# Another order of the steps in the opening of an attention and FFN kernel

## The chip, the cores and the metric

The kernel runs on one core of a Trainium2 chip. The core has engines that work side by side, each on its own row of instructions: TensorE for matmuls (PE in the profile, its weight loads PEld), VectorE (DVE), ScalarE (ACT), GpSimd (POOL) and SyncE (SP), which here only issues DMAs. An engine takes its instructions strictly in the order in which the program lists them; an instruction whose data isn't there yet holds up everything behind it on that engine. The metric is the device time of one launch in microseconds.

## What is computed

Attention with keys and values that are averaged over groups of 8 positions, then layer norm and a feed-forward network with a residual:

```python
B, H, S, D = 8, 8, 576, 64                     # q, k, v in float32
k_p = k.reshape(B, H, S // 8, 8, D).mean(axis=3)
v_p = v.reshape(B, H, S // 8, 8, D).mean(axis=3)
scores = np.matmul(q, k_p.transpose(0, 1, 3, 2)) / np.sqrt(D)
attn = softmax(scores)
x = concat_heads(np.matmul(attn, v_p))         # (8, 576, 512)
xn = (x - mean(x)) / np.sqrt(var(x) + 1e-06) * g_ln
out = x + np.maximum(xn @ w_ch1, 0.0) @ w_ch2  # 512 -> 2048 -> 512
```

## The kernel before

The 4608 tokens are 36 tiles of 128, and four tiles make a chunk of 512 rows of the FFN. Every float32 operand of a matmul is split into two float16 parts, hi and lo, and each product is three matmuls (hi by hi, hi by lo, lo by hi). The first two chunks run the FFN plainly; from the third on a scheme with seven products in place of eight takes over. The weights w1 and w2 arrive as raw 1 MB blocks, eight each, and are made into scaled float16 pairs on the chip. The opening does all of this at once, from about 0 to 230 us: the attention of the first tiles, the making of both weights, the plain FFN of two chunks, and the sums of weights that the seven products need.

What sets the order is written out by hand. Each piece of work is a generator, and a table of tokens drives it: every time that a token appears in the table, its generator runs on to its next `yield` and so adds its next few instructions to the rows of the engines; a token whose generator has ended does nothing.

```python
for token in tokens.split():
    if token not in begun:
        name, *args = token.split(".")
        begun[token] = iter(ops[name](*map(int, args)) or ())
    next(begun[token], None)
```

There are two tables: START for the opening, of some 760 tokens, and STEADY for the rest. The tokens that matter here:

- A.t: scores of tile t (PE L790, maximum and subtraction on DVE L800 and L805, exponentials and float16 parts on ACT L814 to L819 and POOL L826, L829, then a transpose by DMA on SP, L837). E.t.h does the transposing of the first four tiles on PE.
- B.t: attention times values (PE L928 to L930 for the first batch, L932 and L933 later, with `va` and `vb`; sums and statistics on DVE L939 to L961, normalising on POOL L968 and L987, float16 parts and a transpose for the FFN, L1083 to L1090). Tiles 0 to 3 are transposed on PE (L881, L889).
- HV.b.h, HK.b.h: load and average values and keys of a batch. D.b: four DMAs on SP (L757, L758) that spread the values of batch b into `va` and `vb`. HV.1.1's last steps make those values (ACT L483 into `vh`, DVE L490 into `vb`).
- R.m.b: the load of raw block b of weight m (SP L510). C.m.b: its conversion (ACT L535 and L539, DVE L527 and L543; for w2 the maximum on ACT L553). M1.h, M2.h: the scale of half h of a weight (a chain on DVE with one matmul, PE L470).
- S.m.b: the split of block b into float16 hi and lo. It writes over the place of block b - 1, so the splits of a weight form a chain. ACT makes hi (L483); lo is made by DVE (L490), and for S.2.0 to S.2.3 by ACT (L485) and POOL (L487).
- F.c.f (with a third index for the two column halves of the first steps): one block of the FFN's first matmul, 12 matmuls, PE L1116, then ACT L1125 and DVE L1127, which write the hidden activations (`ring`). G.c.t.h: half h of the second matmul for one token tile, 24 matmuls, PE L1319, then DVE L1330. G.0.0.0 needs the splits S.2.0 to S.2.3, one after the other; its last matmuls need S.2.3. G.0.0.1 needs S.2.4 to S.2.7 in the same way.
- T.h.k: sums of blocks of w1 for the seven products (DVE L618, four instructions, L622, L626; POOL L620, L624, L606; ACT L604).

PE's results lie in a pool `ps_f` of three buffers; a step may begin only when the evacuation of the step three before it is done.

## Time and profile before

| | us |
|---|---|
| median of the runs | 790.34 (789.63 to 791.15) |
| profiled execution: span | 789.2 |
| PE busy in it | 772.6 |
| DVE, POOL, ACT busy | 626.3, 486.9, 469.6 |
| PE waits for the first transfer | 6.6 |

The profile is one execution of the program, with times in microseconds from the start of the span. A matmul's end is modelled, so a busy PE is not proof of full speed; the idle time of PE and what ended it are what to read. For each wait the trace names the instruction that released it. The chain that ended last is followed back from the last instruction to what released it, step by step. The other engines have idle time of their own, which costs nothing as long as PE does not wait for them.

### The profile page before, as it was taken

Reading aid. Unit: us, or ns where it says so; the run is one execution under the profiler, and the core shown is the slowest. Engines: PE = TensorE matmul, PEld = TensorE weight load, DVE = VectorE, ACT = ScalarE, POOL = GpSimd, SP = SyncE. Lnnn points to the kernel's source line nnn. Section 1 sums busy time; section 2 is a strip of 40 time slices with the busy share of each in tenths; the row PEclk is TensorE's granted clock in tenths of the full one; section 3 lists DMA queues with packets and bytes.
Section 4 is the critical chain, followed back from the end, with each engine's and each line's share of the span. In section 5 each row is a group of like instructions: output and inputs, shape, how many; then the busy total and the mean of one; then the engine's idle time right before and its main releaser. Section 6 shows DMA issues by size and latency. Waiting matters only on the chain.

```text
span 789.2 us, 18979 instructions
## 1 busy us (share of the span) xinstructions
PE 772.6 (98%) x7458; PEld 593.2 (75%) x7458; DVE 626.3 (79%) x1296; ACT 469.6 (60%) x880; POOL 486.9 (62%) x597
## 2 busy tenths in 40 slices
...
GB/s 352 297 208 228 225 166 106 173 98 44 49 135 164 168 201 189 235 180 228 199 172 204 229 163 268 132 219 189 230 83 209 171 165 161 174 148 147 72 130 134
DMA packets 181513, 139.01 MB, mean 176 GB/s; under 512 B 143792, under 2 KB 151600, under 8 KB 179248
## 3 DMA queue, kind: packets, MB, share of 16 engines
...
q10 hardware_dynamic: 1152, 0.90, 0.4%
...
## 4 chain that ended last, share of the span: by engine, by line
PE 81%; DVE 6%; ACT 6%; POOL 3%; DMA 2%; issue 1%; SPq 0%; POOLq 0%; DVEq 0%; ACTq 0%
PE ps_f L1160 29%; PE ps_f L1277 25%; PE ps_f L1319 14%; PE ps_f L1116 8%; PE ps_a L790 2%; PE ps_a L932 1%; DMA zts<-hl 1%; PE ps_a L933 1%; PE ps_m L723 1%; DVE w L1198 1%; POOL w L487 1%; DVE x L1294 1%; DMA w<-in_kvn_dram 1%; DMA ring<-w2s 1%; ACT w L483 1%
## 5 line engine op out<-in xcount | busy, mean ns | idle before, releaser
L1277 PE MATMUL ps_f<-ring,w 128*128 128x256 f16 x2016 | 231.8, 273 | 1.1 <-DVE x L1294 0.5
L1277 PEld LDWEIGHTS <-w 128*128 128x128 f16 x2016 | 196.1, 98 | 25.6 <-issue 2.0
L1160 PE MATMUL ps_f<-zts,w 128*128 128x256 f16 x1680 | 207.2, 273 | 0.4 <-ACT raw L1179 0.2
L1160 PEld LDWEIGHTS <-w 128*128 128x128 f16 x1680 | 162.9, 98 | 20.4 <-issue 0.8
L1319 PE MATMUL ps_f<-w,ring 128*128 128x512 f16 x576 | 126.8, 379 | 1.3 <-POOL w L487 1.3
L1319 PEld LDWEIGHTS <-ring 128*128 128x128 f16 x576 | 55.9, 98 | 67.1 <-issue 1.6
L1179 ACT COPY raw<-ps_f 128x256 f32<-128x256 f32 x160 | 56.0, 372 | 79.7 <-PE ps_f L1160 69.4
L1160 PE MATMUL ps_f<-zts,tsp 128*128 128x256 f16 x672 | 92.4, 273 | 1.3 <-ACT raw L1179 1.3
L1116 PE MATMUL ps_f<-zts,w 128*128 128x512 f16 (+1 forms) x480 | 85.9, 336 | 1.0 <-DVE ring L1127 1.0
L1196 ACT CAST w<-w 128x512 f16<-128x512 f32 x96 | 59.1, 619 | 38.2 <-POOL w L1219 20.3
L1198 POOL TENSOR_TENSOR w<-w 128x512 f16<-128x512 f32 x48 | 56.8, 1184 | 30.9 <-ACT w L1196 30.8
L1116 PEld LDWEIGHTS <-w 128*128 128x128 f16 x480 | 46.1, 98 | 36.6 <-issue 1.9
L1160 PEld LDWEIGHTS <-tsp 128*128 128x128 f16 x672 | 64.4, 98 | 10.2 <-issue 1.9
L1294 DVE SCALAR_TENSOR_TENSOR x<-ps_f,y,x 128x256 f32<-128x256 f32 (+1 forms) x84 | 42.3, 517 | 34.4 <-PE ps_f L1277 33.5
L826 POOL TENSOR_TENSOR phl<-e,phl 128x512 f16<-128x512 f32 x32 | 39.3, 1227 | 42.4 <-ACT phl L816 34.4
L1215 POOL TENSOR_TENSOR w<-raw 128x256 f32<-128x256 f32 x32 | 24.6, 768 | 56.4 <-ACT raw L1207 38.1
L1085 POOL TENSOR_TENSOR hl<-raw,hl 128x640 f16<-128x640 f32 x28 | 41.9, 1500 | 22.3 <-ACT hl L1083 22.3
L1294 DVE SCALAR_TENSOR_TENSOR x<-ps_f,cy,x 128x256 f32<-128x256 f32 (+1 forms) x84 | 42.2, 515 | 12.8 <-PE ps_f L1277 11.3
L1198 DVE TENSOR_TENSOR w<-raw,w 128x512 f16<-128x512 f32 (+1 forms) x64 | 44.6, 701 | 4.5 <-ACT w L1196 4.2
L1179 ACT COPY phl<-ps_f 128x256 f32<-128x256 f32 x64 | 23.1, 370 | 34.4 <-PE ps_f L1160 33.0
L1174 DVE TENSOR_TENSOR raw<-ps_f,raw 128x256 f32<-128x256 f32 x80 | 32.5, 416 | 9.5 <-PE ps_f L1160 7.5
L1198 DVE TENSOR_TENSOR w<-w 128x512 f16<-128x512 f32 x48 | 36.8, 766 | 4.2 <-ACT w L1196 4.1
...
## 6 DMA issues: line engine op xcount, KB each, us to landing
...
```

The costliest lines, as they stand in the source:

```text
L826: nc.gpsimd.tensor_tensor(out=ph[:, 0, :, KA:P], in0=e[:, :, 0:KA], in1=ph[:, 0, :, 0:KA], op=ALU.subtract)
L1085: nc.gpsimd.tensor_tensor(out=zhl[:, 1, :], in0=src, in1=zhl[:, 0, :], op=ALU.subtract)
L1116: nc.tensor.matmul(ps, lhsT=w[:, part, fs], rhs=zT[:, kz, cols], start=(n == 0), stop=(n == 3 * NKT - 1),)
L1160: nc.tensor.matmul(ps, lhsT=w[:, part, f * P : (f + 1) * P], rhs=z, start=m in (1, 2, 4, 5) and n == 0, stop=m in (2, 3, 4, 7) and n == 3 ...
L1174: nc.vector.tensor_tensor(out=o, in0=ps, in1=o, op=ALU.add)
L1179: nc.scalar.copy(out=o, in_=ps)
L1196: nc.scalar.copy(out=hi, in_=src)
L1198: engine.tensor_tensor(out=lo, in0=src, in1=hi, op=ALU.subtract)
L1215: nc.gpsimd.tensor_tensor(out=s_tmp[:, 0], in0=r01, in1=r11, op=ALU.add)
L1277: nc.tensor.matmul(ps, lhsT=wt[2][:, left, part, f * HC + u * P : f * HC + (u + 1) * P], rhs=b[:, f // FPB, wp, f % FPB], start=n < 4 and ...
L1294: nc.vector.scalar_tensor_tensor(out=x, in0=ps, scalar=scale, in1=x, op0=ALU.mult, op1=ALU.add)
L1319: nc.tensor.matmul(ps, lhsT=h[:, part, i, cols], rhs=w[:, wp, j], start=(n == 0), stop=(n == 3 * NFT // 2 - 1),)
```

## The change

The table START is written anew: the same steps in another order, from its first line to its last. STEADY, and every generator, stay. No instruction is added, removed or moved to another engine; some tokens now stand where their generator has ended already and do nothing. Which of the three `ps_f` buffers a step gets follows the order. Of the 45 lines of the table that differ, a line of before around B.4 and two pairs of after, around B.4 and around T.1.0:

```diff
--- before.py
+++ after.py
@@ -62,45 +62,45 @@
 START = """
...
-C.1.4 F.0.7.0 S.2.3 B.4 B.4 B.4 G.0.0.0 HV.1.1 M1.1 F.0.0.1 F.0.1.1 S.2.3 A.7 F.0.6.1 A.5 A.6 A.6 F.0.7.1 F.0.6.1 R.2.4
...
+F.0.6.1 B.4 E.3.1 F.0.2.1 F.0.1.1 C.1.7 M1.1 A.6 S.2.2 F.0.6.1 F.0.3.1 A.5 A.6 F.0.1.1 S.2.2 C.1.4 HK.2.1 B.4 F.0.7.1
+F.0.1.1 C.1.4 A.6 M1.1 S.2.3 F.0.3.1 B.5 M1.1 F.0.7.1 HK.2.0 B.4 A.8 HV.2.0 E.1.1 A.7 B.5 S.2.3 F.0.3.1 G.0.0.0 C.1.7
...
+HK.2.0 F.0.10 G.0.0.0 A.9 HK.3.0 A.5 M2.1 F.0.14 HV.2.0 F.0.15 HV.2.0 S.2.4 A.8 F.0.10 HV.2.1 S.2.4 S.2.5 F.0.15 T.1.0
+S.2.5 F.0.13 S.2.6 B.5 B.5 F.0.15 S.2.6 B.6 A.10 T.1.0 F.0.13 S.2.7 F.0.13 F.0.15 B.6 T.1.0 R.1.4 F.0.14 R.2.7 A.8 T.1.0
...
 """
```

At the following three places the prediction looks closer. The names are the program's tiles, with numbers that differ from program to program: `w2_91` and `w1_90` are the two weights, `ring_95` the hidden activations, `ps_f` a PSUM buffer.

ACT, around the splits S.2.0 and S.2.1 of the kernel before (each L483 with L485 on `w2_91` is one split; `raw_790` is a raw block of w1 in C.1.4, `vh` the values of HV.1.1):

```order
L483 ACTIVATE w2_91<-w2_91,ws_99 128x1024
L485 ACTIVATE w2_91<-w2_91,ws_99 128x1024
L1125 ACTIVATE ring_95<-ps_f_893 128x256
L535 ACTIVATE w1_90<-raw_790 128x1024
L539 ACTIVATE raw_790<-raw_790 128x1024
L1125 ACTIVATE ring_95<-ps_f_921 128x256
L483 ACTIVATE vh_976<-vp_260,sv_975 72x8x64
L483 ACTIVATE w2_91<-w2_91,ws_99 128x1024
L485 ACTIVATE w2_91<-w2_91,ws_99 128x1024
```

ACT, around S.2.2 and S.2.3 of the changed kernel (`raw_695` is the same raw block, in C.1.4):

```order
L483 ACTIVATE w2_91<-w2_91,ws_99 128x1024
L485 ACTIVATE w2_91<-w2_91,ws_99 128x1024
L1125 ACTIVATE ring_95<-ps_f_1066 128x256
L535 ACTIVATE w1_90<-raw_695 128x1024
L539 ACTIVATE raw_695<-raw_695 128x1024
L483 ACTIVATE w2_91<-w2_91,ws_99 128x1024
L485 ACTIVATE w2_91<-w2_91,ws_99 128x1024
```

The conversion C.1.4 (L535, L539) stood between S.2.0 and S.2.1, and stands between S.2.2 and S.2.3 now.

PE, where B.4 begins, before (`pt` are its transposed exponentials, `va` and `vb` the spread values; `ps_f_1081` is F.0.7.1):

```order
L1116 MATMUL ps_f_1081<-zts_94,w1_90 128x256
L932 LDWEIGHTS pt_846
L932 MATMUL ps_a_1102<-va_208,pt_846 64x65
L933 LDWEIGHTS pt_846
L933 MATMUL ps_a_1102<-vb_209,pt_846 64x65
```

PE, where B.4 begins, after (`ps_f_996` is F.0.6.1, `ps_a_1010` the scores of A.7):

```order
L1116 MATMUL ps_f_996<-zts_94,w1_90 128x256
L790 MATMUL ps_a_1010<-kblk1_114,q_705 64x72 x16
L932 LDWEIGHTS pt_868
L932 MATMUL ps_a_1032<-va_212,pt_868 64x65
L933 LDWEIGHTS pt_868
```

B.4 came last, behind the last F step of the column halves; now it follows A.7, and three of those F steps (F.0.1.1, F.0.3.1, F.0.7.1), then M1.1 and B.5, stand between it and G.0.0.0. Before, G.0.0.0 followed B.4 directly, and M1.1 and B.5 came behind G.0.0.0. B.4's L987 on POOL, which stood behind the last L487, now stands in front of it.

SP's queue in the same stretch, before (L510 loads raw blocks of w1, the transpose is A.4's, and the last four are D.1):

```order
L510 DMA raw_790<-in_w1_dram 128x2048
L510 DMA raw_833<-in_w1_dram 128x2048
L775 DMA q_835<-in_qT_dram 128x512
L659 DMA vr_840<-in_v_dram 72x512
L510 DMA tsp0_92<-in_w1_dram 128x2048
L510 DMA tsp1_93<-in_w1_dram 128x2048
L837 DMA_TRANSPOSE pt_846<-phl0_115 128x16x128
L775 DMA q_938<-in_qT_dram 128x512
L757 DMA va_977<-vh_976 64x520
L758 DMA vb_978<-vh_976 8x520
L757 DMA va_977<-vh_976 64x520
L758 DMA vb_978<-vh_976 8x520
```

SP's queue, after:

```order
L510 DMA raw_807<-in_w1_dram 128x2048
L659 DMA vr_814<-in_v_dram 72x512
L510 DMA tsp0_92<-in_w1_dram 128x2048
L837 DMA_TRANSPOSE pt_868<-phl0_115 128x16x128
L659 DMA vr_874<-in_v_dram 72x512
L510 DMA tsp1_93<-in_w1_dram 128x2048
L775 DMA q_951<-in_qT_dram 128x512
L757 DMA va_957<-vh_956 64x520
L758 DMA vb_958<-vh_956 8x520
L757 DMA va_957<-vh_956 64x520
L758 DMA vb_958<-vh_956 8x520
```

Of the four loads of raw blocks ahead of the transpose, one stood further up already (R.1.4, not in the rows), two are still there, and one, into `tsp1_93`, stands behind it.

DVE, around the splits S.2.4 to S.2.7 (L490), before:

```order
L1127 SCALAR_TENSOR_TENSOR ring_95<-ps_f_1441,ring_95 128x512
L490 SCALAR_TENSOR_TENSOR w2_91<-w2_91,ws_99 128x1024
L1127 SCALAR_TENSOR_TENSOR ring_95<-ps_f_1498,ring_95 128x512
L490 SCALAR_TENSOR_TENSOR w2_91<-w2_91,ws_99 128x1024
L1127 SCALAR_TENSOR_TENSOR ring_95<-ps_f_1552,ring_95 128x512
L490 SCALAR_TENSOR_TENSOR w2_91<-w2_91,ws_99 128x1024
L1127 SCALAR_TENSOR_TENSOR ring_95<-ps_f_1574,ring_95 128x512
L490 SCALAR_TENSOR_TENSOR w2_91<-w2_91,ws_99 128x1024
L1127 SCALAR_TENSOR_TENSOR ring_95<-ps_f_1597,ring_95 128x512
```

DVE, the same place, after (`raw_1634` holds the sums of T.1.0):

```order
L1127 SCALAR_TENSOR_TENSOR ring_95<-ps_f_1514,ring_95 128x512
L490 SCALAR_TENSOR_TENSOR w2_91<-w2_91,ws_99 128x1024
L618 TENSOR_TENSOR raw_1634<-w1_90 128x512 x4
L490 SCALAR_TENSOR_TENSOR w2_91<-w2_91,ws_99 128x1024
L1127 SCALAR_TENSOR_TENSOR ring_95<-ps_f_1607,ring_95 128x512
L490 SCALAR_TENSOR_TENSOR w2_91<-w2_91,ws_99 128x1024
L1127 SCALAR_TENSOR_TENSOR ring_95<-ps_f_1641,ring_95 128x512
L622 TENSOR_TENSOR raw_1634<-raw_1634 128x512
L490 SCALAR_TENSOR_TENSOR w2_91<-w2_91,ws_99 128x1024
L1127 SCALAR_TENSOR_TENSOR ring_95<-ps_f_1592,ring_95 128x512
```

Four sums of T.1.0 (L618) now stand between S.2.4 and S.2.5, and its L622 ahead of S.2.7, where there were only the evacuations of F steps (L1127); before, T.1.0 came behind G.0.0.1.

## Rows read from the trace of the kernel before

**Rows 1.** The page: span, and part 1: engine, busy us, share of the span, instructions.

```profile
span 789.2 us, 18979 instructions
...
PE 772.6 (98%) x7458; PEld 593.2 (75%) x7458; DVE 626.3 (79%) x1296; ACT 469.6 (60%) x880; POOL 486.9 (62%) x597
```

**Rows 2.** Waits of PE: line waited for, us in total, times, longest us.

```profile
PE ps_m L723 <- DMA w<-in_kvn_dram: 6.6, 1, 6.6
...
PE ps_f L1319 <- POOL w L487: 1.3, 1, 1.3
PE ps_f L1116 <- DVE ring L1127: 1.0, 3, 0.4
PE ps_m L877 <- ACT z L902: 0.7, 1, 0.7
PE ps_a L929 <- POOL pt L867: 0.6, 1, 0.6
```

**Rows 3.** The chain that ended last, 70 to 90 us: start us, us, what.

```profile
70.33 2.14 POOL w L487
...
75.00 2.11 POOL w L487
...
79.61 2.15 POOL w L487
...
81.80 1.24 PE ps_f L1319 x5
...
83.61 6.48 PE ps_f L1319 x30
```

**Rows 4.** Timeline of ACT, 64 to 67 us: start us, us, instruction.

```profile
64.91 1.14 ACT L535 ACTIVATE w<-raw 128x1024 f32<-128x1024 f32 x1
65.95 1.14 ACT L539 ACTIVATE raw<-raw 128x1024 int32<-128x1024 uint16 x1
```

**Rows 5.** Timeline of POOL, 64 to 84 us; in brackets the idle time before.

```profile
64.81 2.14 POOL L487 TENSOR_TENSOR w<-w 128x1024 f16<-128x1024 f32 x1 [0.21 <-ACT w L485]
...
81.98 2.07 POOL L987 TENSOR_SCALAR z<-x,ln 128x512 f32<-128x512 f32 x1
```

**Rows 6.** Timeline of DVE, 79 to 82 us.

```profile
79.42 0.23 DVE L940 TENSOR_SCALAR sm<-ps_a,cvm 128x8 f32<-128x8 f32 x1
...
81.38 0.18 DVE L961 BATCH_NORM_AGGREGATE ln<-st 128x2 f32<-128x6 f32 x1
```

**Rows 7.** Timeline of SP's queue, 57 to 73 us.

```profile
57.34 1.71 SPq L510 DMA_DIRECT2D tsp<-in_w_dram  x2
59.14 9.71 SPq L837 DMA_TRANSPOSE pt<-phl  x1
...
71.39 0.68 SPq L758 DMA_DIRECT2D vb<-vh  x1
```

**Rows 8.** Timeline of PE, 66 to 81 us.

```profile
66.72 4.10 PE L1116 MATMUL ps_f<-zts,w 128*128 128x256 f16 x36
...
76.19 4.27 PE L1319 MATMUL ps_f<-w,ring 128*128 128x512 f16 x19
```

**Rows 9.** Timeline of DVE, 115 to 126 us.

```profile
115.45 1.28 DVE L490 SCALAR_TENSOR_TENSOR w<-w,ws 128x1024 f16<-128x1024 f32 x1 [0.69 <-ACT w L483]
...
123.35 1.32 DVE L490 SCALAR_TENSOR_TENSOR w<-w,ws 128x1024 f16<-128x1024 f32 x1 [0.61 <-ACT w L483]
124.59 0.68 DVE L1127 SCALAR_TENSOR_TENSOR ring<-ps_f,ring 128x512 f16<-128x512 f32 x1
```

**Rows 10.** Timeline of PE, 118 to 126 us.

```profile
121.57 4.70 PE L1319 MATMUL ps_f<-w,ring 128*128 128x512 f16 x21
```

**Rows 11.** Groups by line and form: ns min/median/max, first and last start us.

```profile
L490 DVE SCALAR_TENSOR_TENSOR w<-w,gs x8: 1272/1277/2456, 30.4 to 100.0; 128x1024 f16<-128x1024 f32 x8
...
L618 DVE TENSOR_TENSOR raw<-w x16: 675/681/1207, 136.7 to 187.4; 128x512 f32<-128x512 f16 x16
...
L867 POOL TENSOR_TENSOR pt<-phl,pt x8: 1152/1160/2130, 17.9 to 42.8; 72x512 f16<-72x512 f32 x8
```

73 lines of the change are left out of this document (35 added, 38 removed).

## The prediction

> **What bounds the kernel now.** I read the page first: the span is 789.2 us and TensorE (PE) is busy 772.6 of it [rows 1]. The 7458 matmuls are the same in both kernels, so only the 16.6 us in which PE stands idle can change, by shrinking or by growing. Next the waits of PE: 6.6 us go to the first transfer, before any order can matter, and the rest is in small pieces, of which I quote those of the opening, 1.3, 1.0, 0.7 and 0.6 us [rows 2]. Added up over the opening, what is not the first transfer comes to some 4 us, and that is the most a new order can win there. What it can lose has no such limit, since the same order could make new waits.
>
> Then the chain that ended last, around its largest piece. There the reader is to see ACT and POOL alternating through the splitting of the second weight matrix: POOL's half of a split takes 2.1 us, and its starts come at 70.33, 75.00 and 79.61, 4.6 us apart. Each split overwrites what the one before it read, so they can't overlap. The last ends at 81.75, PE's last five matmuls of G.0.0.0 start at 81.80, and PE is past B.5 at 83.61 [rows 3]. From there on PE runs dense until about 230 us.
>
> **Which edits matter.** The changed table permutes the opening's steps; the second table, which runs from about 230 us to the end, is the same. I followed each engine's new row with the durations of the old trace. Most moves end where they began: PE has other work in front of it. Four terms are left.
>
> **First 48 us: even.** Two waits of PE are there, 0.6 us in B.0 and 0.7 us in B.2 [rows 2]. E.0.1 now comes ahead of a matmul of V0, and E.1 must wait for stage A.1's maximum behind two converts on DVE, about 0.9 us, while B.0's 0.6 goes. B.2 on the other side loses at most its 0.7, and may get as much back, because four DVE steps now stand ahead of the values that its last matmuls read. I take 0; bounds -0.7 to +0.7.
>
> **The splits of w2 and the step that needs them: -1.5 us.** Before, convert C.1.4 stood on ACT between the first and the second split: two instructions of 1.14 us [rows 4]. That stretched the first step from 64.81 [rows 5] to 70.33, 5.5 us where the others take 4.6: 0.9 us lost. In the new row C.1.4 stands between the third and the fourth split, where ACT must wait out POOL's 2.1 us anyway, so that only some 0.3 us of it sticks out. The chain also starts about 0.4 us earlier, since M2.0 comes a little sooner in the row. That makes -0.9 - 0.4 + 0.3 = -1.0: the last split ends near 80.75. One more thing stands ahead of it now: POOL's 2.07 us for B.4 (L987) [rows 5], which needs B.4's statistics on DVE, 2.1 us from L940 to L961 [rows 6]. By my chain they are done at 75.7, B.4 itself having ended by 73, and POOL is free of L987 at about 78.3, when ACT's part of the last split is done too. So it fits, with almost nothing to spare.
>
> PE's own path has also changed. B.4, which stood behind three F steps, now stands ahead of them, and M1.1 and B.5 stand ahead of G.0.0.0. So 0.6 us of work (M1.1 and B.5, from the end of G.0.0.0 at 83.04 to 83.61, [rows 3]) that came behind the wait now lies under it. But B.4's second half needs the spread copies of its values, D.1, which are issued on SP. Before, the transpose of A.4 held SP from 59.14 for 9.7 us, behind two 1 MB loads, and the last piece of D.1 was issued by 72.07 [rows 7]. Now one of these loads (R.1.7) stands behind the transpose, and the transpose starts near 57.5; D.1 then waits for its data instead, ready at 68.1 on DVE, and takes the same 2.5 us to issue, to 70.6. Its landing is not shown, because nobody waited for it; 0 us after the last issue is one end, 3.6 us (when B.4's second half ran) the other, and I take 1.2: 71.8. PE would get there at 70.2, so it stands 1.6 us, which it could afford: after the landing it has 0.5 (half of B.4), 4.0 (36 matmuls of F, [rows 8]), 0.6 and 24 matmuls at 0.216 us (30 take 6.48, [rows 3]), 5.2: together 10.3, which ends at 82.1. The splits' path ends at 80.75 + 1.24 = 82.0 [rows 3]. The later one counts: 82.1 against 83.61, a gain of 1.5 us. Ends: 1.6 us (landing early) and a loss, priced below.
>
> **G.0.0.1: +0.4 us.** Before, splits five to eight ran on ACT and DVE from 115.45 (the first L490) to 124.67, and the last values F wrote were ready at 125.3 [rows 9]; PE began G.0.0.1 at 121.57 [rows 10] and needed the last split 19 matmuls later, at 125.7. Nobody waited. Now T.1.0's four sums (L618, 0.68 us each, [rows 11]) stand on DVE between the fifth and the sixth split, and its L622 (0.7 us) ahead of the eighth. Step by step: 1.3 + 2.8 + 1.3 to the end of the sixth, 1.2 + 1.3 for the seventh, then 1.4 for an evacuation and L622 (ACT's 1.15 lies beside it), 1.3 for the eighth: 10.6 us where it took 9.2. PE comes about 0.85 us later to this place, counted from M2.1, because A.9 now stands before it. Slack for the eighth split 1.0 + 0.85 - 1.4 = 0.45; for F.0.14's values behind it about -0.15. Bounds of the wait: 0, and 1.5 us if one L490 and one L618 take their longest (+1.2 and +0.5, [rows 11]) over a slack of 0.2; I take 0.4, nearer the low end, which the plain durations give.
>
> How DVE and POOL get on with each other decides the upper end. The grouped rows show L490 at 1.28 us in the median and 2.46 at most, POOL's L867 at 1.16 and 2.13, and L618 at 0.68 and 1.21 [rows 11]; so an instruction can take about twice its time where the other engine works beside it. The Trainium skill, "SBUF — State Buffer", section "SBUF: two separate sides", says why: a DVE instruction with two SBUF inputs and a GpSimd instruction share a port pair, and whichever starts first holds it for the whole instruction. This case's longest durations agree; by that rule T.1.0's four sums, which now run beside POOL's L987 and L1085, could cost DVE one or two such instructions and the sum would be about 790.3 instead (an estimate, inside the same band, with the upper end of the wait in place of 0.4).
>
> **Everything else: 0.** F.1.0 on the new order needs B.7's transposed half at about 144.5 and gets it about 2 us earlier; F.1.3 and G.1.0.0 have 0.5 to 0.8 us to spare. I leave these at nothing; if a cover fails, each costs some tenths.
>
> **Sum.** 0 - 1.5 + 0.4 = -1.1 us against the profiled span of 789.2, so 788.1. The median of the runs, 790.34, lies 1.1 us over the span; with that, **789.2 us**. A measurement here can tell about 0.2% from no change, that is 1.6 us: the forecast is a gain too small to be told.
>
> **The rivals.**
> *A clear gain.* The splits end at 80.4, D.1 lands by 71, nothing waits in G.0.0.1, and B.2's 0.7 us goes: -1.6 - 0.5 = -2.1, 788.2. For it: all pieces sit on named waits. Against: L987 leaves no room ahead of the last split, and the idle time in the opening is 4 us in all. Chance 0.27.
>
> *Slower: B.4 comes too early.* If the transpose of A.4 holds SP 9.7 us again, R.1.7 is issued only at 67.3, directly ahead of D.1, and its 1 MB lies in the queues in front of the four spreads. PE now has nothing ahead of B.4 to fill the time, as it had in the three F steps. Each us of landing later than 71.8 costs one us; the gain is gone at 83.61 - 10.3 = 73.3, and from 74.9 on (74.5 with G.0.0.1's 0.4) the kernel is slower by over 0.2%. B.4's statistics, L987 and the last split move along. A landing at 74.8 gives +1.5, and with G.0.0.1's 0.4 that is 792.2. For it: the trace shows exactly such a transpose [rows 7]. Against: it had two more 1 MB loads in front of it than it has now. Chance 0.15, with a further 0.07 for a wait in G.0.0.1 or F.1 beyond 2 us, through the same DVE row.
>
> *No gain, no loss.* L987 slips ahead of the last split by a us (B.4's statistics late), so the splits end at 81.7 as before, and G.0.0.1 takes back the 0.6 that B.5 and M1.1 give: 790.2. It lies within the forecast's own band. Forecast and this one together: 0.51.
>
> **How the numbers follow.** Faster by over 0.2% (under 788.8): 0.27. Within: 0.51. Slower (over 791.9): 0.22. The range reaches from half a us under the clear gain, 787.6, since other pieces of the 4 us idle may go too, to a landing of the spreads near 75 with G.0.0.1's wait, 792.4; about 0.1 is left out at each end.
>
> **What the changed profile would show.** Right: PE's wait in G.0.0.0 for POOL's L487 is under 1 us or gone, the last L487 ends near 80.8, PE waits 1 to 2 us inside B.4, and is at the start of dense work near 82.3. C.1.4's two ACT instructions lie under POOL's third split. Right for the second term: a wait of some tenths in G.0.0.1. Wrong: an idle stretch of PE over 3 us before B.4's second half, a split that ends after 81.8, a new wait of over 1 us between 120 and 160 us, or a wait behind 250 us that before did not have.

## The result, and the profile after

The changed kernel takes 798.45 us in the median (798.28 to 799.57), the kernel before 790.17 beside it: a ratio of 1.0107 [1.0092, 1.0121]. It is 8.3 us slower, where I had forecast a gain of 1.1 and a range up to 792.4. The profiled executions differ by 7.4 us in their spans, 796.6 against 789.2 [rows 1].

The page of the kernel after, its first part:

```profile
span 796.6 us, 18975 instructions
...
PE 776.0 (97%) x7458; PEld 594.0 (75%) x7458; DVE 636.4 (80%) x1296; ACT 470.1 (59%) x880; POOL 496.7 (62%) x597
```

The instructions are the same, and ACT needs the same time for them. DVE needs 10.1 us more than in [rows 1], POOL 9.8 more, PE 3.4 more. Nothing was added, so single instructions took longer. The waits of PE after (line waited for, us in total, times, longest):

```profile
PE ps_m L723 <- DMA w<-in_kvn_dram: 6.2, 1, 6.2
PE ps_a L932 <- DVE x L950: 1.6, 2, 0.9
PE ps_a L929 <- POOL pt L867: 1.4, 1, 1.4
...
PE ps_a L932 <- DMA vb<-vh: 1.2, 1, 1.2
PE ps_f L1319 <- DVE ring L1127: 1.0, 3, 0.5
PE ps_f L1319 <- POOL w L487: 0.8, 1, 0.8
```

Against [rows 2], three of over 1 us are new: for `x` (L950), for the spread values (`vb`), and a longer one for `pt` (L867). To see where the time went I took, for each step of PE, the time from its start to the start of the next step in both traces, and counted what is over the smaller of the two:

| stretch of PE | after less before, us |
|---|---|
| up to B.2 (about 48 us) | -0.1 |
| B.3 with its wait, and the half clock behind it | +3.1 |
| waits of before for evacuations of F.0, 62 to 71 us | -1.2 |
| B.4's second half | +1.8 |
| M1.1 and B.5, up to the start of G.0.0.0 | +1.5 |
| G.0.0.0 | -0.5 |
| F.0.8 and others behind 90 us | +0.3 |
| F.0.13 and G.0.0.1 | +1.5 |
| G.0.3.1 and F.1.0 | +0.5 |
| B.9 (in V.10's place), 163 us | +1.1 |

Together that is about 8 us; the two spans differ by 7.4, since the wait for the first transfer, which the table leaves out, was 0.4 us shorter in this execution (6.2 against 6.6), and the rest is rounding. Nothing is lost or won behind 235 us. So there is no one culprit: some 5 of the 8 us go between 50 and 87 us, the rest in small pieces up to 165 us.

**The first piece, B.3.** POOL's timeline after, 44 to 52 us, then DVE's, then PE's (idle time before an instruction in brackets):

```profile
45.57 1.35 POOL L670 TENSOR_TENSOR vr<-vr 72x128 f32<-72x128 f32 x1
47.00 0.32 POOL L671 TENSOR_TENSOR vp<-vr 72x64 f32<-72x64 f32 x1
47.28 4.23 POOL L867 TENSOR_TENSOR pt<-phl,pt 72x512 f16<-72x512 f32 x2
```

```profile
45.35 1.25 DVE L490 SCALAR_TENSOR_TENSOR w<-w,gs 128x1024 f16<-128x1024 f32 x1
...
47.18 1.22 DVE L543 SCALAR_TENSOR_TENSOR w<-w,raw 128x1024 int32<-128x1024 int32 x1
48.32 2.18 DVE L543 SCALAR_TENSOR_TENSOR w<-w,tsp 128x1024 int32<-128x1024 int32 x1
```

```profile
51.57 0.20 PE L929 MATMUL ps_a<-vh,pt 72*128 72x65 f16 x1 [1.45 <-POOL pt L867]
...
52.30 2.75 PE L1116 MATMUL ps_f<-zts,w 128*128 128x256 f16 x12
```

Two L867, 1.16 us each in the median [rows 11], took 4.23. They took turns with DVE's two L543: the first L867 begins when the first L543 has 1.1 us to go and ends at 49.41, the second L543 takes 2.18 in place of 1.22 and ends at 50.50, and the second L867 ends 1.0 after that, at 51.51. PE starts at 51.57. Behind this wait the 12 matmuls of F.0.4.0 take 2.75 us instead of 1.47. The windows of the kernel after say why (the first two columns are the length and PE's busy time, the last three the granted clock, the share of the DMA engines and GB/s):

```profile
50.00:52.00 2.00, 0.55 (x18) 0.43 (x15) 1.97 (x4) 2.00 (x4) 2.00 (x2) 1.00 0.99 416
52.00:54.00 2.00, 2.00 (x21) 1.47 (x18) 1.90 (x6) 1.97 (x3) 1.76 (x5) 0.51 0.74 263
54.00:56.00 2.00, 2.00 (x39) 1.37 (x38) 1.79 (x3) 2.00 (x5) 1.92 (x4) 0.63 0.03 5
```

PE was busy for 0.55 us of the 2 us before, and then ran at the lower of its two levels (granted clock 0.51, that is 1.2 GHz of 2.4) for more than 2 us. In this execution a wait of 1.45 us cost about 3.

The half clock doesn't come each time. Eight of the profiled kernels have the changed order unaltered up to here; six of them wait 1.44 to 1.46 us at this place, and in this one alone the clock fell behind it. One of the others is the kernel with its two copies on ACT, below (L931 and L1118 are L929 and L1116 there):

```profile
51.38 0.20 PE L931 MATMUL ps_a<-vh,pt 72*128 72x65 f16 x1 [1.44 <-POOL pt L866]
...
51.99 1.47 PE L1118 MATMUL ps_f<-zts,w 128*128 128x256 f16 x12
```

From the end of the wait to the next transposes on PE (L881, in that kernel L880) it is 6.91 us in the kernel after and 5.31 in that one: the clock's part of the 3.1 us is 1.6. An execution of the kernel after with a mean granted clock of 1.0 took 798.54 us, so the loss as a whole doesn't come from the clock.

**The second, B.4 to G.0.0.0.** PE after, 70 to 90 us, then POOL and DVE in the same stretch:

```profile
74.33 0.22 PE L932 MATMUL ps_a<-va,pt 128*64 128x65 f16 x1 [1.18 <-DMA vb<-vh]
...
80.11 0.19 PE L932 MATMUL ps_a<-va,pt 128*128 128x65 f16 x1 [0.67 <-DVE x L950]
81.27 4.26 PE L1319 MATMUL ps_f<-w,ring 128*128 128x512 f16 x19 [0.48 <-DVE ring L1127]
86.37 1.24 PE L1319 MATMUL ps_f<-w,ring 128*128 128x512 f16 x5 [0.84 <-POOL w L487]
```

```profile
66.83 2.12 POOL L487 TENSOR_TENSOR w<-w 128x1024 f16<-128x1024 f32 x1 [0.59 <-ACT w L485]
71.56 2.14 POOL L487 TENSOR_TENSOR w<-w 128x1024 f16<-128x1024 f32 x1 [2.49 <-ACT w L485]
76.50 2.14 POOL L487 TENSOR_TENSOR w<-w 128x1024 f16<-128x1024 f32 x1 [1.07 <-ACT w L485]
81.10 3.11 POOL L987 TENSOR_SCALAR z<-x,ln 128x512 f32<-128x512 f32 x1 [2.19 <-DVE ln L961]
84.19 2.13 POOL L487 TENSOR_TENSOR w<-w 128x1024 f16<-128x1024 f32 x1
```

```profile
76.47 2.20 DVE L939 COPY cvm<-cv 64x3 f32<-64x3 f32 x2
78.78 0.23 DVE L940 TENSOR_SCALAR sm<-ps_a,cvm 128x8 f32<-128x8 f32 x1
...
80.73 0.18 DVE L961 BATCH_NORM_AGGREGATE ln<-st 128x2 f32<-128x6 f32 x1
81.14 1.22 DVE L543 SCALAR_TENSOR_TENSOR w<-w,raw 128x1024 int32<-128x1024 int32 x1
```

SP gave out D.1's last spread at 71.08 to 71.76, and B.4's second half starts at 74.33: 2.6 us later. Then B.4's two copies of a 64x3 tile (L939), 0.16 us each in the median, take 2.20: the second takes 2.04 of it and ends at 78.67, when L487 ends at 78.64. Before, on DVE:

```profile
78.99 0.33 DVE L939 COPY cvm<-cv 64x3 f32<-64x3 f32 x2
```

So B.4's statistics end at 80.91, L987 starts at 81.10, is itself held (3.11, against 2.07 in [rows 5], with an L543 on DVE beside it), and only then comes the last L487, for which ACT had been ready since 81.45. It ends at 86.32; I had 80.75.

**The third, G.0.0.1.** DVE after, 119 to 133 us; [rows 9] are its counterpart:

```profile
119.78 1.45 DVE L490 SCALAR_TENSOR_TENSOR w<-w,ws 128x1024 f16<-128x1024 f32 x1 [0.62 <-ACT w L483]
121.15 3.73 DVE L618 TENSOR_TENSOR raw<-w 128x512 f32<-128x512 f16 x4
124.80 1.62 DVE L490 SCALAR_TENSOR_TENSOR w<-w,ws 128x1024 f16<-128x1024 f32 x1
...
129.51 1.04 DVE L622 TENSOR_TENSOR raw<-raw 128x512 f32<-128x512 f32 x1
130.47 1.32 DVE L490 SCALAR_TENSOR_TENSOR w<-w,ws 128x1024 f16<-128x1024 f32 x1
```

From the fifth split to the end of the eighth it is 12.0 us, where I had 10.6: the four sums took 3.73 in place of 2.7 (one of them 1.92, beside POOL's L671 and L1085), an L490 1.62 in place of 1.28, L622 1.04 in place of 0.68. All 16 L618 of the program take 15.8 us after and 10.8 before.

### The profile page after: what moved, and what is told of

Read it like the earlier page. It is cut to its first block, busy times and chain, and to the rows that moved or that the text cites. A ratio compares the mean times of both kernels' runs of the same rounds, so it can differ in the third digit from the quotient of the medians.

```text
span 796.6 us, 18975 instructions
## 1 busy us (share of the span) xinstructions
PE 776.0 (97%) x7458; PEld 594.0 (75%) x7458; DVE 636.4 (80%) x1296; ACT 470.1 (59%) x880; POOL 496.7 (62%) x597
## 4 chain that ended last, share of the span: by engine, by line
PE 72%; DVE 13%; POOL 7%; DMA 3%; ACT 2%; issue 1%; SPq 1%; DVEq 0%; POOLq 0%; ACTq 0%
PE ps_f L1160 29%; PE ps_f L1277 25%; PE ps_f L1319 9%; PE ps_f L1116 5%; PE ps_a L790 2%; DVE wm L527 1%; DMA kr<-in_kT_dram 1%; DVE raw L618 1%; DMA zts<-hl 1%; PE ps_a L932 1%; POOL pt L867 1%; PE ps_m L723 1%; PE ps_a L933 1%; DVE w L1198 1%; DVE mx L800 1%
## 5 line engine op out<-in xcount | busy, mean ns | idle before, releaser
L1116 PE MATMUL ps_f<-zts,w 128*128 128x512 f16 (+1 forms) x480 | 86.9, 340 | 0.5 <-DVE x L1330 0.3
L1116 PEld LDWEIGHTS <-w 128*128 128x128 f16 x480 | 46.9, 99 | 38.2 <-issue 2.2
L1160 PEld LDWEIGHTS <-tsp 128*128 128x128 f16 x672 | 64.3, 98 | 10.1 <-issue 1.6
L1085 POOL TENSOR_TENSOR hl<-raw,hl 128x640 f16<-128x640 f32 x28 | 41.9, 1500 | 27.6 <-ACT hl L1083 27.6
L1179 ACT COPY phl<-ps_f 128x256 f32<-128x256 f32 x64 | 23.2, 370 | 34.3 <-PE ps_f L1160 33.0
L1125 ACT ACTIVATE ring<-ps_f 128x512 f16<-128x512 f32 (+1 forms) x40 | 19.5, 506 | 39.4 <-PE ps_f L1116 33.4
```

The source lines that it names most:

```text
L1085: nc.gpsimd.tensor_tensor(out=zhl[:, 1, :], in0=src, in1=zhl[:, 0, :], op=ALU.subtract)
L1116: nc.tensor.matmul(ps, lhsT=w[:, part, fs], rhs=zT[:, kz, cols], start=(n == 0), stop=(n == 3 * NKT - 1),)
L1160: nc.tensor.matmul(ps, lhsT=w[:, part, f * P : (f + 1) * P], rhs=z, start=m in (1, 2, 4, 5) and n == 0, stop=m in (2, 3, 4, 7) and n == 3 ...
L1179: nc.scalar.copy(out=o, in_=ps)
```

## The experiments

A token table is changed in all but three of them; the diffs show the tokens at the place, with the table's line ends left out. Medians stand beside 790.1 to 790.8 of the kernel before on the same chip. In a few kernels the line numbers of the trace are one to three off; the text says so where it matters.

### The three pieces, one by one

**B.3: E.3's POOL steps ahead of one averaging.**

```diff
-HV.1.0 B.2 ... F.0.0.0 C.2.1 E.3.0 E.3.1 F.0.1.0
+E.3.0 E.3.1 HV.1.0 B.2 ... F.0.0.0 C.2.1 F.0.1.0
```

> The changed kernel with one edit: the two POOL steps of E.3 (L867, which B.3 waits for) stand ahead of one HV.1.0 pooling step (three instructions, 2.5 us in the trace after) instead of behind it. Theory (B.3's wait of 1.45 us comes from POOL's row, and the 3.3 us at half clock right behind it are a consequence of that wait): the wait and the stretch at 0.50 both go, some 3 us less than the changed kernel, 795.4 us. Rival 1 (the low clock has another cause): the wait goes, the stretch at half clock stays, 797.0. Rival 2 (what PE gains there it waits for later, at the splits): 798 or more.

Measured: 800.33 us, 1.0127 [1.0108, 1.0146], slower still. The wait in B.3 is gone; PE waits instead 0.97 in B.2, and 2.34 at 67.94 for an evacuation, since the later averaging holds up a load on SP and all loads behind it. There the clock falls to 0.53. That B.3 waited for POOL's row is seen in the trace after, where L867 releases PE. This run doesn't show which step was one too many, since two kernels below that change nothing up to here (B.4 behind F.0.1.1, and R.1.7 behind D.1) also wait 0.97 in B.2 and not in B.3. What it shows is that the row had no room to give: the averaging that was put off is missed later.

**B.3: the step of PE behind F.0.4.0.**

```diff
-C.2.2 B.3 F.0.4.0 B.2
+C.2.2 F.0.4.0 B.3 B.2
```

> The changed kernel with one step of PE moved: B.3's matmuls stand behind F.0.4.0's (12 matmuls, 1.3 us) instead of ahead of them. No step of POOL, DVE, ACT or SP moves. Theory (B.3's 1.45 us are plain waiting for POOL, which other work can cover): the wait shrinks to some tenths, and the half clock that followed it in the first trace does not come: 1.3 us less than the changed kernel without the clock, up to 2.8 with it, 795.6 to 797.1. Rival (as when POOL's step was moved ahead: something behind it then comes late instead, a load on SP or an evacuation on DVE): 798 or more.

Measured: 797.2 us, 1.0085. The wait and the half clock are gone, 3 us at this place. PE gets to B.4's second half 3.3 us earlier, but the spreads land only 2.3 us earlier, and it waits 2.14 there in place of 1.18:

```profile
72.01 0.22 PE L932 MATMUL ps_a<-va,pt 128*64 128x65 f16 x1 [2.14 <-DMA vb<-vh]
```

In the profiled execution nearly all of it came through: the last five matmuls of G.0.0.0 start at 83.37 in place of 86.37, and the span is 793.9 against 796.6. By the medians it is 1.25 us, with executions from 795.65 to 798.73 and a ratio of [1.0069, 1.0101], which overlaps that of the kernel after; how much of the 3 us this repair gives back is not settled.

**B.4: its two copies (L939) on ACT.**

```diff
+            if t == TPC:
+                for r, b in segs:
+                    nc.scalar.copy(out=cv[r], in_=CV[b][r])
...
-        if len(segs) > 1:
+        if len(segs) > 1 and t != TPC:
```

> The changed kernel with B.4's two tiny copies (L939, 2.05 us for the second in the trace after, 0.17 before) issued on ACT ahead of B.4's matmuls instead of on DVE. Theory (DVE is held by POOL's L487, which ran from 76.51 to 78.65 while the copy ended at 78.67): L940 starts about 2 us earlier, B.5's wait of 0.67 us for L950 goes, POOL's L987 and with it the last L487 come 1.5 to 2.5 us earlier, 1 to 2 us less than the changed kernel, 796.5 to 797.5. Rival (the copy waited for data): L940 stays where it was, 798.4. Third possibility: the next DVE instruction takes over the wait for L487 (L940 or L950), and nothing is gained, 798.4, with that instruction at about 2 us.

Measured: 795.98 us, 1.0064, so 2.5 us better. In this kernel's trace the copies are L919 on ACT, and L942 is L940 of the others. ACT, then DVE:

```profile
70.40 0.39 ACT L919 COPY cvm<-cv 64x3 f32<-64x3 f32 x2
```

```profile
74.65 0.22 DVE L942 TENSOR_SCALAR sm<-ps_a,cvm 128x8 f32<-128x8 f32 x1
```

The statistics begin at 74.65 instead of 78.78, B.5 doesn't wait, and the last split ends at 82.69 instead of 86.32. Of these 3.6 us, 1.8 stood at the first split already (65.03 against 66.83), as the clock didn't fall behind B.3 in this execution; the other 1.8 is what two tiny copies behind a 2.1 us instruction of POOL had cost the splits. So that cause is shown; what it is worth in the whole lies between 1 and 2.5 us. L987 (L989 here) still takes 3.05, and PE waits 0.82 for the last split.

**B.4 as a whole behind F.0.1.1.**

```diff
-F.0.6.1 B.4 E.3.1 F.0.2.1 F.0.1.1 C.1.7
+F.0.6.1 E.3.1 F.0.2.1 F.0.1.1 B.4 C.1.7
```

> The changed kernel with B.4's matmuls behind F.0.1.1's instead of ahead of them; no other engine's row changes. Theory (B.4 stands before its spread values land, 1.4 to 1.8 us of idle PE): the idle time shrinks to some tenths, but B.5 then waits longer for DVE's L950 and G.0.0.0 for POOL's L487, which do not move: PE gains less than 0.5 us by the end of G.0.0.0, 798.0 to 798.5. Rival (B.4 is what sets the end of G.0.0.0): 1.3 us less, 797.1.

Measured: 798.56 us, 1.0096, no gain. B.4 stands 0.3 us where it stood 1.18, and B.5 waits 1.69 for L950 where it waited 0.67. PE's wait for the spreads was cover for DVE's lateness. In this execution PE also waits 0.97 in B.2 and not at all in B.3, though nothing is changed up to there: which of POOL and DVE comes first at 45 us differs from one execution to the next.

**G.0.0.1 and B.9: the sums T behind them.**

```diff
-S.2.5 F.0.15 T.1.0 S.2.5 ... T.1.0 F.0.13 S.2.7 ... T.1.0 R.1.4 ... T.1.0 S.2.7 F.0.14 HV.2.1
+S.2.5 F.0.15 S.2.5 ... F.0.13 S.2.7 ... R.1.4 ... S.2.7 F.0.14 T.1.0 T.1.0 T.1.0 T.1.0 HV.2.1
...
-F.1.1 T.1.1 T.0.0 T.0.0 F.1.1 ... B.0 B.9 A.11
+F.1.1 T.1.1 F.1.1 ... B.0 B.9 T.0.0 T.0.0 A.11
```

> The changed kernel with T.1.0's first four steps moved behind S.2.7 and F.0.14's evacuation, and T.0.0's first two behind B.9's DVE step. Theory (the sums stand in DVE's row ahead of what PE needs): G.0.0.1's waits (0.74 us named, 1.06 us longer than its 5.34) go, and the 0.94 us that V.10 waits for B.9's L950 go: 1.6 to 2.4 us less, about 796.4. Rival (the sums are only put off, and the steps behind them, up to the first product step, then wait for them): the waits move to F.1.0 or V.10 or the start of the products, 798 or more.

Measured: 803.63 us, 1.0161. In G.0.0.1 0.36 us of the loss is left, so the sums were its cause; but the work of DVE that went behind makes waits of 2.57 and 2.20 at A.10 (139 and 142 us) and two more at 171 and 178 (0.58 and 1.29). Five us more were lost than won.

### Whole stretches

**Before's order from M2.1 on.** The first 346 tokens of the changed table, then before's in their order, without those that have stood.

```diff
 HK.2.1 A.7
-G.0.3.0 HK.1.1 F.0.10 HK.2.0 HK.3.0 F.0.9 HV.2.1 R.2.6 HV.2.1 M2.1 F.0.12
...
+LN.2 LK.1 ... G.0.3.0 S.1.4 F.0.9 F.0.10 F.0.9 F.0.8 G.0.2.0 C.2.5 F.0.10 A.5 C.1.7 B.6 C.2.7
```

> The changed kernel's order up to M2.1 (about 115 us), and from there the order of the kernel before for all that is left of the opening. Theory (from M2.1 on the new order loses 3.1 us by the milestones of PE, 4.3 us are lost ahead of it): 3 us less than the changed kernel, 795.4. Rival (the late part loses only because it starts with POOL and DVE behind, so any order would lose there): less than 1 us gained, 797.5 to 798.5.

Measured: 795.55 us, 1.0056. What I had costed at +0.4 and 0 behind M2.1 costs 2.9 us, and it is gone with the old order there.

**Before's order up to F.0.0.0.**

```diff
 B.3 F.0.0.0
-F.0.0.0 F.0.0.0 F.0.0.0 F.0.1.0 F.0.1.0 F.0.1.0 C.2.3
+HV.1.1 HV.1.1 F.0.0.0 F.0.1.0 F.0.0.0 HV.1.1 A.4 C.2.2
...
```

(here the minus lines are before's table)

> The order of the kernel before up to F.0.0.0 (about 47 us), and from there that of the changed kernel for all that is left of the opening. Theory (the first loss, B.3's wait, comes from the first 48 us, which the prediction called even): it goes, the later ones stay, 795.4 to 797. Rival (the losses behind it are made by the state that the first part leaves, POOL and SP behind): all of the middle's loss goes too, under 794.5.

Measured: 799.93 us, 1.0113. I had expected the first loss to go. B.3's wait did, but at the joint new ones came: 2.0 at A.5, 0.98 at a scale, 2.66 for the spreads, with the clock at 0.65 behind it. A stretch of an order rests on the state of the queues with which the stretch before hands over, so this says little on either order by itself.

### DVE and POOL: two of the three additions of the averaging taken out of both kernels

```diff
-        nc.gpsimd.tensor_add(out=vr[:, 0:4, :], in0=vr[:, 0:4, :], in1=vr[:, 4:8, :])
-        nc.gpsimd.tensor_add(out=vr[:, 0:2, :], in0=vr[:, 0:2, :], in1=vr[:, 2:4, :])
```

These kernels leave out two of the three additions by which POOL averages the values, so their averages are not those of the task; the order stays.

> The changed kernel without the first two of the three additions of each pooling step of values on POOL (L669 and L670; the third, L671, stays), in all 16 such steps of batches 1 and 2, so that the values are wrong. That takes some 20 us of work off POOL's row, and what it holds of DVE; order, loads and all other instructions stay. Theory (the new order's losses in the opening come from DVE and POOL holding each other up, at places where it left no room): B.3's wait goes, instructions of DVE and POOL that took twice their time come back to it, 3 to 5 us less than the changed kernel, 793.5 to 795.5, while the kernel before, cut in the same way, gains 1 us at most. Rival (the losses come from the order of the rows as such, whatever each takes): both gain the same, and the changed kernel stays 7 to 8 us behind the kernel before.

> The kernel before without the same additions (L669 and L670), as a measure for the run of the changed kernel without them. Theory: its waits of PE in the opening are 4 us in all and few of them hang on POOL, so 0 to 1 us less than before, 789.5 to 790.5. Rival (POOL's work costs both kernels alike): 3 us less or more, 787.5.

Measured: after 794.37 us (1.0048), before 791.08 (1.0008). The same 32 instructions of POOL are worth 4.1 us in the one and nothing in the other, and the gap falls from 8.3 to 3.3 us. The pages, first of after without them, then of before without them:

```profile
PE 773.8 (98%) x7458; PEld 594.3 (75%) x7458; DVE 630.7 (80%) x1296; ACT 470.3 (59%) x880; POOL 468.6 (59%) x565
```

```profile
PE 772.2 (98%) x7458; PEld 593.2 (75%) x7458; DVE 627.6 (79%) x1296; ACT 469.8 (59%) x880; POOL 463.7 (59%) x565
```

DVE, on which nothing was taken away, falls from 636.4 to 630.7 in the changed order and stays (626.3, 627.6) in the old one. So more than half of the loss hangs on this load of POOL. There are two ways for it to do so, and these runs don't part them: POOL's row is 28.1 us shorter (23.2 in the old order), so that POOL is simply earlier, and DVE and POOL hold each other up less. DVE's 5.7 us speak for the second. The wait in B.4 stays (2.43, with the clock at 0.50 behind it): that one is the transfers' own.

### The 1 MB load in front of the spreads

**R.1.7 behind D.1,** with C.1.7's maximum and M1.1's chain, which need it, behind B.4's statistics.

```diff
-S.2.0 R.1.7 C.1.4 ... D.1 F.0.7.0 ... F.0.1.1 C.1.7 M1.1 A.6 ... B.4 F.0.7.1
+S.2.0 C.1.4 ... D.1 R.1.7 F.0.7.0 ... F.0.1.1 A.6 ... B.4 C.1.7 M1.1 F.0.7.1
```

> The changed kernel with the 1 MB load R.1.7 issued behind D.1's four spreads instead of ahead of them, and with what reads it, C.1.7's maximum (L527) and the chain of M1.1 on DVE, behind B.4's DVE step. Theory (the spreads land 2.6 us after the last issue because that load's packets lie in front of them): they land about 1 us after it, B.4's wait of 1.2 to 1.8 us shrinks to some tenths, and B.4's copies (L939) no longer meet POOL's third split, so B.5's wait goes as well: 1.5 to 3 us less than the changed kernel, 795.5 to 797. Rival 1 (the spreads are slow by themselves): B.4 waits as before, only the copies' 2 us go, 797. Rival 2 (the weights made later than now cost more): F.0.8, which needs block 7 of w1, waits over 1 us, 798 or more.

Measured: 799.52 us, 1.0113. SP's queue in this kernel:

```profile
70.39 0.68 SPq L758 DMA_DIRECT2D vb<-vh  x1
71.11 0.43 SPq L510 DMA_DIRECT2D tsp<-in_w_dram  x1
71.59 5.59 SPq L837 DMA_TRANSPOSE pt<-phl  x1
```

and PE's next wait:

```profile
80.00 0.23 PE L470 MATMUL ps_m<-ident,rowmax 128*128 128x128 bf16 x1 [2.96 <-DVE rowmax L439]
```

B.4 doesn't wait any more: the last spread is issued by 71.07 and the second half runs from about 72.2, so a landing takes 1.2 us at most without the load in front, against 2.6 with it (3.3 in the kernel with B.3 later). The single packets in the traces agree: in the kernel after the spreads' run until 73.48, with R.1.7's among them until 72.05; here they end at 71.89, and R.1.7's first comes at 72.17. But the load is late for M1.1, which waits 2.96. My 1.2 us for the landing was right for an empty queue, and the queue wasn't empty.

**All of these together:** R.1.7 and M1.1 behind, B.3 later, copies on ACT, before's order from M2.1.

```diff
-C.2.2 B.3 F.0.4.0 ... S.2.0 R.1.7 C.1.4 ... B.5 M1.1 F.0.7.1 ... G.0.0.0 C.1.7
+C.2.2 F.0.4.0 B.3 ... S.2.0 C.1.4 ... B.5 F.0.7.1 ... G.0.0.0 M1.1 M1.1 C.1.7
...
```

> All edits that helped, in one: the changed kernel's order up to M2.1 with B.3 behind F.0.4.0, the two copies of B.4 on ACT, the load R.1.7 behind D.1's spreads, C.1.7's maximum and M1.1's chain behind B.4 on DVE, and M1.1's matmul behind G.0.0.0 (as before) instead of ahead of it, so that nobody waits for the chain; from M2.1 on the order of the kernel before. Theory (the losses are separate and each has been named): PE waits under 1 us between 48 and 100 us, 788.5 to 790.5, as fast as the kernel before or up to 2 us faster. Rival (each move takes away a cover somewhere else, as the load behind the spreads did for M1.1, so that the sum of the edits is less than the edits): 792 or more, with a new wait of over 1 us that none of the runs so far had.

Measured: 796.19 us, 1.0089. One large wait is left: 3.56 in B.5 for the transpose of A.5, which now stands behind R.1.7 on SP.

**Without touching R.1.7:** B.3 later, copies on ACT, B.4 behind F.0.1.1, before's order from M2.1; the diffs are those above.

```diff
-C.2.2 B.3 F.0.4.0 B.2 ... F.0.6.1 B.4 E.3.1 F.0.2.1 F.0.1.1 C.1.7
+C.2.2 F.0.4.0 B.3 B.2 ... F.0.6.1 E.3.1 F.0.2.1 F.0.1.1 B.4 C.1.7
...
```

> Four edits in one: the changed kernel's order with the two copies of B.4 on ACT, B.3 behind F.0.4.0, B.4 behind F.0.1.1, and from M2.1 on the order of the kernel before. Theory (the four losses are separate: 1.5 to 3 us at B.3, 2 to 2.5 at the copies, 0.5 to 1.4 at B.4, 3 from M2.1 on): 7 to 9 us less than the changed kernel, 789.5 to 791.5, as fast as the kernel before or a little faster. Rival (they share a cause, so that the gains overlap): 793 or more.

Measured: 792.64 us (790.89 to 796.79), 1.0033 [1.0017, 1.0049]. This is the best of the new orders, and still not faster than the old one. B.4 waits 2.07 in it:

```profile
74.81 0.22 PE L935 MATMUL ps_a<-va,pt 128*64 128x65 f16 x1 [2.07 <-DMA va<-vh]
```

(L935 is L932 of the others.) The last spread was issued by 70.10 and landed 4.7 us later, the longest of all. R.1.7's last packet ended at 70.95 and the spreads' last at 72.37, so 2.4 of the 4.7 us lie behind the last packet (0.85 in the kernel after); what filled them, no run here shows.

### B.4, M1.1 and B.5 back in their old places

**B.4's first two steps behind the F steps, M1.1 and B.5 behind G.0.0.0.**

```diff
-F.0.6.1 B.4 E.3.1 ... HK.2.1 B.4 F.0.7.1 F.0.1.1 C.1.4 A.6 M1.1 S.2.3 F.0.3.1 B.5 M1.1 ... A.7 B.5 S.2.3 F.0.3.1 G.0.0.0 C.1.7
+F.0.6.1 E.3.1 ... HK.2.1 F.0.7.1 F.0.1.1 B.4 B.4 C.1.4 A.6 S.2.3 F.0.3.1 ... A.7 S.2.3 F.0.3.1 G.0.0.0 M1.1 B.5 M1.1 B.5 C.1.7
```

> The changed kernel with B.4's matmuls behind the three F steps, and M1.1 and B.5 behind G.0.0.0, as in the kernel before (with the DVE steps that read them moved along; POOL, ACT and SP keep the changed order). Theory (these three steps stand too early on PE, whatever delays the transfers): no wait of PE inside B.4 or B.5, 1.5 to 2.5 us less than the changed kernel, 796 to 797. Rival (G.0.0.0 is set by POOL's last split in any case, behind B.4's L987, which now comes later still): the whole wait shows up as PE waiting for L487, 798 to 800.

Measured: 802.33 us (800.17 to 804.32), 1.0156. B.4 doesn't wait, an evacuation behind M1.1's chain costs 1.11, and G.0.0.0 waits:

```profile
83.99 2.10 PE L1319 MATMUL ps_f<-w,ring 128*128 128x512 f16 x5 [3.18 <-POOL w L487]
```

and behind it five matmuls take 2.10 us instead of 1.24 (clock 0.55). L987 stands ahead of the last L487 (POOL 78.97 to 81.83), idle 2.42 us before it for B.4's statistics. B.6 then waits 1.37 for B.5's L950.

**The same with B.3 later, copies on ACT and before's order from M2.1.**

```diff
-C.2.2 B.3 F.0.4.0 B.2
+C.2.2 F.0.4.0 B.3 B.2
...
```

> The same, and B.3 behind F.0.4.0, the two copies on ACT, and from M2.1 on the order of the kernel before. Theory (the four losses, at B.3, at B.4 to G.0.0.0, at the copies and from M2.1 on, add up to the 8 us): 789.5 to 791.5, level with the kernel before. Rival (a part of the loss has not been found, or the last split is late because of L987): 793 or more.

Measured: 798.3 us, 1.0100, with the same three waits (1.11, 3.25 for L487, and 1.37 in B.6).

**L987 behind the last split too,** where before has it.

```diff
-F.0.7.1 HK.2.0 B.4 A.8 ... A.7 S.2.3 F.0.3.1
+F.0.7.1 HK.2.0 A.8 ... A.7 S.2.3 B.4 F.0.3.1
```

> e14_places_back (the changed order, with B.4's matmuls and statistics behind the F steps, and M1.1 and B.5 behind G.0.0.0), and now B.4's third step (POOL L968 and L987) also behind the last split's L487, where before has it. Theory (the 3.2 us wait in G.0.0.0 of that kernel came because L987 stood ahead of the last L487 and so tied G.0.0.0 to B.4's statistics): that wait falls below 1 us and its stretch at the half clock goes, so 802.3 falls by 3 to 4.5, to 798 or 799; the 1.1 us at the evacuation behind M1.1's chain stays. Rival (the last split was late of itself): the wait stays over 2 us, 801 to 803.

Measured: 800.28 us (799.05 to 801.77), 1.0121, between the two expectations. G.0.0.0's wait for L487 is gone, so it was L987 that had tied the split to B.4. But now B.6 waits for B.5's L950, as PE's timeline shows, with POOL's and DVE's behind it:

```profile
87.61 0.21 PE L932 MATMUL ps_a<-va,pt 128*128 128x65 f16 x1 [3.41 <-DVE x L950]
```

```profile
80.19 2.14 POOL L487 TENSOR_TENSOR w<-w 128x1024 f16<-128x1024 f32 x1 [2.51 <-ACT w L485]
```

```profile
80.27 3.15 DVE L543 SCALAR_TENSOR_TENSOR w<-w,raw 128x1024 int32<-128x1024 int32 x1
```

L543, 1.2 us elsewhere, starts 0.08 behind L487, and ends 1.09 behind L487's end at 82.33. B.5's statistics stand further down the same row; its L950 starts at 86.77. The clock falls to 0.50 behind the wait and eats the rest.

### The predicted gain, made by itself on the old order

**Through the values of HV.1.1:** their L483 on ACT behind the second split instead of ahead of it, with what hangs on it, and A.7's DVE step behind two evacuations.

```diff
-HV.1.1 C.1.4 HV.1.1 HV.1.1 C.2.3 D.1 D.1 R.1.6 F.0.3.1 F.0.4.1 M2.0 S.2.1 F.0.3.1 F.0.2.1 C.1.7 F.0.3.1
+C.1.4 C.2.3 R.1.6 F.0.3.1 F.0.4.1 M2.0 S.2.1 C.1.7 HV.1.1 HV.1.1 HV.1.1 D.1 D.1 F.0.3.1 F.0.2.1 F.0.3.1
...
-A.7 F.0.6.1 A.5 A.6 A.6 F.0.7.1 F.0.6.1 R.2.4
+F.0.6.1 A.5 A.6 A.6 F.0.7.1 F.0.6.1 A.7 R.2.4
```

> The order of before, with one half of the predicted gain made by itself in another way: in the stretch of the first split of w2, ACT makes the values of HV.1.1 (L483, 72x512, 0.62 us) behind the second split's two instructions instead of ahead of them (C.1.7's L527 on DVE goes ahead of the L490 that follows, D.1 behind), and A.7's maximum and subtraction on DVE (L800, L805) go behind the two evacuations of F.0.7.1 and F.0.6.1. PE's row and POOL's row stay as they are. Theory (the 1.3 us wait in G.0.0.0 is winnable where nothing else is moved): the last L487 ends 0.6 us earlier, PE's wait for it falls from 1.3 to about 0.7, and the time falls by 0.6: 789.5. Rival (the cover is gone): D.1 is issued 1.0 us later, its last spread by 73.1, and with a landing of 2.6 us it is there at 75.7, where B.4's second half asks for it at 75.2: a new wait of 0.5 there, no gain: 790.1.

Measured: 790.69 us beside 790.56, 1.0001 [0.9991, 1.0011]: no difference, as the rival had it, though by another wait. The last split ends at 80.44 and the wait for it is gone. DVE, then PE:

```profile
69.53 2.17 DVE L490 SCALAR_TENSOR_TENSOR vb<-vp,sv,vh 72x512 f16<-72x512 f32 x1
```

```profile
72.08 4.09 PE L1116 MATMUL ps_f<-zts,w 128*128 128x256 f16 x36 [1.80 <-DVE ring L1127]
```

The L490 of the values, 0.74 us before, now begins 0.50 behind an L487 that lasts to 71.15, takes 2.17, and the evacuations behind it are late. Before, PE waited 0.29 here and 1.33 for the split, together 1.62; now it waits 1.80 here.

**Through C.1.4,** as the changed table has it: L535 and L539 behind S.2.2, and A.6's and A.7's steps out of their way.

```diff
-A.7 C.1.4 F.0.2.1 ... HV.1.1 C.1.4 HV.1.1 ... F.0.5.1 F.0.4.1 A.6 S.2.3 ... F.0.7.1 A.6 C.1.4 F.0.7.0 S.2.3 B.4
+A.7 F.0.2.1 ... HV.1.1 HV.1.1 ... F.0.5.1 C.1.4 F.0.4.1 S.2.3 ... F.0.7.1 C.1.4 F.0.7.0 S.2.3 A.6 B.4
...
```

> The order of before, with the edit that the prediction gave 0.9 us, done alone: C.1.4's two instructions on ACT (L535, L539) go from between the splits S.2.0 and S.2.1 to between S.2.2 and S.2.3; what stood there (A.6's exponentials on ACT, their part on POOL) goes behind S.2.3, C.1.4's L543 on DVE behind C.1.5's conversion, and A.7's maximum and subtraction behind the evacuations of F.0.7.1 and F.0.6.1. Theory (each piece of the gain was there, and was lost to the other moves of the new table): the last L487 ends about 1 us earlier, near 80.7, the wait in G.0.0.0 is under 0.4 us, and the time falls by 0.9: 789.2. Rival (a single move shifts the wait): A.6's transpose goes out on SP some 4 us later, its POOL part stands in front of B.4's L987, and what stands behind them waits: the wait in G.0.0.0 goes but comes back as one or two of 0.5 to 1 us up to 110 us: 790 to 791.

Measured: 793.74 us, 1.0039 [1.0025, 1.0053], slower than either expectation. The wait for the last L487 is 1.5, not under 0.4. ACT, with C.1.4 away:

```profile
65.71 0.38 ACT L1125 ACTIVATE ring<-ps_f 128x256 f16<-128x256 f32 x1 [1.12 <-PE ps_f L1116]
67.20 0.72 ACT L483 ACTIVATE vh<-vp,sv 72x512 f16<-72x512 f32 x1 [1.11 <-POOL vb L749]
67.83 1.13 ACT L483 ACTIVATE w<-w,ws 128x1024 f16<-128x1024 f32 x1
```

The second split starts no earlier: the evacuation ahead of it waits for PE and the values' L483 for POOL (a fill of `vb` that stands behind an L487). C.1.4 had filled 2.2 us in which ACT would have stood idle. Most of the 0.9 us that I gave to this move isn't there in the old order. New waits of 0.54, 0.39 and 1.09 between 100 and 105 us make the loss; I haven't taken them apart.

## Why the prediction was wrong

**"Four terms are left."** This step failed first. I had followed each engine's new row with the durations of the old trace and dropped every place where the engine seemed to have work in front of it. Two of the places that I dropped, B.3 and B.9, cost 4.2 us in the profiled execution, 1.6 of them the half clock. What I had used as fixed, the durations, depends on the order: the same instructions took 10 us more on DVE and 10 on POOL.

**"First 48 us: even."** Right to 0.1 us by the account, with other parts: B.0's wait is gone, one of 0.7 at E.1 came. The loss comes 3 us later, at B.3, whose POOL work I had not followed past B.2.

**The splits and the step that needs them: -1.5.** It was +2.8 (1.8 + 1.5 - 0.5). Four sizes in it were off. The landing of D.1's spreads was 2.6 us and not 1.2, since R.1.7's 1 MB had been issued at 66.05, ahead of them. B.4's copies took 2.20 us, not 0.3. L987 took 3.11, not 2.07, and stood ahead of the last split with nothing to spare, as I had written; the last split ended 5.6 us later than forecast, of which 2.4 was there at the first already (66.83, where I had 64.4: B.3's loss) and 2.7 came with L987. That L987 came late was in part the copies' doing. And B.5 needs the place in PSUM from which L950 reads B.4's result: that wait (0.67) I had overlooked when I counted 0.6 us of M1.1 and B.5 as work that lies under the wait. The splits' own first steps did come out nearly as counted, 4.73 and 4.94 us apart. On the old order, though, moving C.1.4 alone gives nothing.

**G.0.0.1: +0.4.** The mechanism was right, the size was not: 1.5 us. The upper bound of the wait, for one L490 and one L618 at their longest, was 1.5, and it came, by luck of the sum: one L618 took 1.92, longer than the longest row that I had (1.21), one L490 1.62 and L622 1.04, the others no longer than 1.45. The nearest rows were the medians of a stretch in which DVE and POOL met less, and I took the low end from them. The Trainium skill, "SBUF — State Buffer", section "SBUF: two separate sides", says that a DVE instruction with two SBUF inputs and a GpSimd instruction shut each other out for a whole instruction. The traces agree, and more widely than I had used it: an L543 ended 1.09 us behind the L487 that held it, and even a 64x3 copy ended with the L487 beside it. I had let this rule move one term by a us; it belonged on every row of DVE and POOL.

**"Everything else: 0."** +1.9: F.0.8 0.3, F.1.0 0.5, B.9 1.1 (four L618 of T.0.0 from 158.57 to 162.18 stand ahead of its L940). Against it stands -1.2 that I hadn't looked for: waits of before for evacuations of F.0, between 62 and 71 us, are gone.

**The rivals.** "Slower: B.4 comes too early" had the right place and cause, and the landing of about 74.3 lay between its two points, 73.3 and 74.9. Its condition came only in part: A.4's transpose held SP for 7.6 us, not 9.7, and that was enough to put R.1.7 ahead of D.1. But it was one of four losses, and I had given it one loss's price. "A clear gain" rested on the idle 4 us of the opening: where I tried to fetch them on the old order, 790.69 and 793.74 came out.

**What I said would show it wrong:** a split that ends after 81.8 (86.32) did; the new wait of over 1 us between 120 and 160 us did not come (0.94 at 163), nor an idle stretch over 3 us in B.4, nor a loss behind 250 us. Two of the signs of being right came as written, a wait under 1 us for the last L487 (0.84) and one of 1 to 2 us inside B.4 (1.18), while both places stood 5.6 and 2.5 us later than forecast: a wait tells nothing of when its place is reached.

**What stays open.** More than half of the 8.3 us hangs on POOL's load, by the pair of kernels with less of it; 2.9 lie behind M2.1, and about 3 in B.3's stretch, and these overlap. How much of POOL's part is its being held by DVE, and how much its being late, is open. The sum can't be split further, since by the medians each single repair gave back less than its piece (1.25 of 3.1, 0 of 1.8, -5 of 1.5), except perhaps the copies (up to 2.5).
